# Block-causal attention, MLP and gated convolution on one core: normalization moved behind the value matmul, MLP begun three half pairs earlier

## The chip, the cores and the metric

The kernel runs on one NeuronCore of a Trainium2 chip. The metric is device time in microseconds (us) of one execution. TensorE (PE in the rows; PEld is its weight load) multiplies matrices into PSUM, VectorE is DVE, ScalarE is ACT, GpSimd is POOL, and SP issues most transfers.

## The reference

Three layers follow each other. All outputs of one are inputs of the next.

```python
# attention: B=8, H=8, S=576, D=64, blocks of 64 keys
scores = scale * np.matmul(q, k.transpose(0, 1, 3, 2))
scores = np.where(block_i >= block_j, scores, -1000000000.0)
attn = np.exp(scores - np.max(scores, axis=-1, keepdims=True))
attn = attn / (np.sum(attn, axis=-1, keepdims=True) + 1e-09)
x = np.matmul(attn, v)                    # heads side by side: 8 x 576 x 512
# MLP, with a token mix of rank 32 ahead of it
u = x + (x.transpose(0, 2, 1) @ U @ V).transpose(0, 2, 1)
x = u + np.maximum(u @ w_ch1, 0.0) @ w_ch2          # 512 -> 2048 -> 512
# gate: causal convolution of 5 taps per channel
gate = 1.0 / (1.0 + np.exp(-gate_pre))
out = (gate * (x @ w_val)) @ w_out
```

The weights are float64, q, k and v are float32.

## The kernel before

*Precision.* A product that must be near fp32 is made of three one-pass products of fp32r parts (high x high, high x low, low x high). `hi_act` and `lo` make such parts. Attention matmuls of the first heads are plain fp32.

*Weight conversions.* `split_w1` and `split_w2` fetch a 512 KB piece of a float64 weight (two staging buffers), join its two words by four VectorE operations (lines 122, 124, 125 and 143), and split the result on ScalarE and GpSimd (lines 91 and 97). There are 32. During the first part of the program one is issued every 12 steps; what is left is issued in MLP group 0, four at its first slice and two at each that follows. Pieces of `w_ch2` go back to DRAM and are loaded again per slice.

*The stream of attention.* `attention()` is a generator whose steps the main loop takes one by one. Its first 16 heads (batches 0 and 1) run in 16 half-pair *slots*. A pair is two heads of a batch; `z` holds the pair's queries block-diagonally, so that a 128-column block `i` of it gives, in one matmul against the keys `tk`, the scores of 64 queries of either head. Half 0 of a pair has the query blocks 6 to 8, half 1 the blocks 0 to 5. In `slot(u)`:

- `emit_q_bank(u, b)` for b = 0, 1, 2 makes the scores of a PSUM tile (line 445), their row maxima on VectorE (447), scales these by -1/8 (459), and lets ScalarE take the exponentials with their row sums (463). Block 8 has 576 keys and lies in two tiles, so its first tile waits for the maximum of the second.
- `emit_q_norm(u)` adds 1e-9 (473), takes reciprocals (474), and multiplies the rows of exponentials by them (479): blocks 0 to 5 on VectorE, 6, 7 and 8 on GpSimd.
- `emit_q_turn(u - 1, b)` turns the normalized rows with TensorE (500) and copies them to SBUF on ScalarE (503).
- `emit_q_pv(u - 2, part)` multiplies the values by them (526), part 0 between banks 0 and 1, part 1 between banks 1 and 2; ScalarE copies the result, the pair's transposed output `xt`, from PSUM (534).
- `mix_T`, `mix_G` and `mix_H2` turn `xt` and add the token mix; they make `uh` and `ul`, which the MLP reads.

From head 16 on, `tick(n)` handles one late head: scores with keys on partitions (`emit_s_piece`, 406), maxima over partitions and a subtraction (593 to 631), exponentials (655), and two ticks later the values (`emit_pv`, 719). From `FIRST_SPLIT` on, a head's exponentials are split into high and low parts (`emit_est`); these use pools that open when all conversions are issued (`open_late`).

*The MLP.* 4608 tokens are nine groups of 512, each of 16 slices of the 2048 hidden features. A slice is 12 matmuls of 512 columns for the hidden layer (946), ScalarE's ReLU and VectorE's remainder (974, 975), and 12 matmuls into four accumulators (998). Group g needs the outputs of batches 0 to g. After every six MLP matmuls `gap()` may take steps from the attention stream; `aim(g)` sets how many, by a count of steps over 60 of the group's 64 gaps. Where the stream yields true, a group's share ends; if it has not come by the group's end, the rest is taken at once, without MLP work between (lines 1192 to 1194).

*Where the MLP begins.* With `BREAK = 15`, slots 0 to 15 run ahead of it. Group 0 then carries the 12 steps that finish pairs 6 and 7; from group 1 on the late heads run between the MLP's matmuls.

*What sets the order.* TensorE's order is that of the program. The other engines' order is chosen by the scheduler, in which parts marked `high_priority` go first. Score tiles and half of the transposed tiles share a ring of four PSUM buffers, tag `a`, before the MLP; inside the MLP a single ring of four holds these, the value tiles, the mix and the hidden layer.

Of the kernel before, what the change touches and what calls it, by code (L numbers as in the profile page):

```python
# [17 lines left out]
P = 128  # L18
# [4 lines left out]
def attn_moe_gate_kernel(ctx: ExitStack, tc: tile.TileContext, q, k, v, U, V, w1, w2, wval, convw, wout, out):  # L23
# [21 lines left out]
    FIRST_SPLIT = 2 * H  # L45
# [31 lines left out]
    BREAK = 2 * H - 1  # L77
    ONVEC = (0, 1, 2, 3, 4, 5)
# [142 lines left out]
    make_identity(nc, ident)  # L221
    unit = const.tile([KC, KC], F32, name="unit")
# [171 lines left out]
    def emit_s_piece(pn, i):  # L394
# [15 lines left out]
        for n, t in zip(heads, ps):  # L410
# [23 lines left out]
    def emit_q_bank(u, b):  # L434

        pn, g = divmod(u, 2)
        z, tk = qkt[pn]
        if b == 0:
            t = tiny_p.tile([P, 24], F32, tag="rq", name="rq")
            halves[u] = [t[:, 6 * c:6 * c + 6] for c in range(4)] + [None]  # L440
        r, nm, l, _, wait = halves[u]
        ps = psum["a"].tile([P, 512], F32, tag="a", name="pS")
        todo = qbanks[g][b]
        for i, k0, k1, o, c in todo:
            pe.matmul(ps[:, o:o + k1 - k0], z[:, i * P:(i + 1) * P], tk[:, k0:k1], start=True, stop=True)
        for i, k0, k1, o, c in todo:
            vec.reduce_max(r[:, c:c + 1], ps[:, o:o + k1 - k0], axis=AX.X)
        if g == 0 and b == 0:
            halves[u][4] = ps
            return  # L450
        c0, c1 = todo[0][4], todo[-1][4] + 1
        todo = [(ps, x) for x in todo]
        if wait is not None:
            vec.tensor_tensor(r[:, 0:1], r[:, 0:1], r[:, 1:2], op=ALU.max)
            vec.tensor_copy(r[:, 1:2], r[:, 0:1])
            c0 = 0
            todo = [(wait, qbanks[0][0][0])] + todo
# [35 lines left out]
    def emit_q_turn(u, b):  # L493
# [9 lines left out]
        act.copy(e, ps[:, 0:c])  # L503
        turned[u, b] = e

    def emit_q_pv(u, part):

        pn, g = divmod(u, 2)
        if part == 0 and g == 0:
            xts[pn] = x_p.tile([P, S], F32, tag="xt", name="xt")  # L510
        xt = xts[pn]
        i0, i1 = half_i[g]
        if part == 0:
            turned[u] = ps_p.tile([P, 512], F32, tag="a", name="pPV")
# [18 lines left out]
        if part == 1:  # L533
            act.copy(xt[:, i0 * D:i1 * D], turned.pop(u)[:, 0:(i1 - i0) * D])
            last[0] = (own[0], xt[own[0]][0:1, i0 * D:i0 * D + 1])

    def slot(u):
# [32 lines left out]
        for step, delay in ((mix_H2, 6), (mix_G, 5), (mix_T, 4)):  # L570
            pn, off = divmod(u - delay, 2)
            if off == 0 and 0 <= pn < 2 * NP:
# [3 lines left out]
                yield u >= NQ and step is mix_H2 and pn == 2 * NP - 1  # L576
# [308 lines left out]
    def attention():  # L885
# [10 lines left out]
        for n in range(NQ, NH + DEPTH + HPOS // 2):  # L896
            yield from tick(n, 2 * NP)
# [375 lines left out]
```

## Time and profile before

| | us |
|---|---|
| median of 3 runs (1484.11 to 1488.53) | 1486.95 |
| the profiled execution | 1485.87 |
| its span, first to last instruction | 1484.0 |
| TensorE busy | 1405.5 (95%) |
| VectorE busy | 1054.6 (71%) |
| ScalarE busy | 702.2 (47%) |
| GpSimd busy | 329.3 (22%) |

A busy share is a mean over stages with different limits. Matmuls overlap, so their durations add up to more than the busy time. In the program the first hidden-layer matmul starts at 162.2 us, group 1 begins at about 280 us and group 2 at about 441 us.

### The profile page before, as it was taken

The page shows a single profiled execution, that of the slowest core. Times are in us where ns is not written, and L with a number is a line of the kernel's source. Part 1 is how long each engine was busy: PE and PEld are TensorE (multiplying, and loading weights), DVE is VectorE, ACT ScalarE, POOL GpSimd, SP SyncE. Part 2 cuts the span into 40 slices and gives each one's busy share as a digit, 9 for nine tenths or more (in the row PEclk, how much of TensorE's full clock was granted, in tenths as well). Part 3 has the DMA queues.
Part 4 walks back from the last instruction along what each step waited for, and adds up shares of the span by engine and source line. Part 5 has one row for each costly group of instructions (what it writes and reads, how often), then busy time and mean ns, then how long its engine had stood idle before and what let it go on. Part 6 is the DMA issues. An engine that isn't in the chain of part 4 may idle for free.

```text
span 1484.0 us, 20191 instructions
## 1 busy us (share of the span) xinstructions
PE 1405.5 (95%) x6736; PEld 1087.3 (73%) x6736; DVE 1054.6 (71%) x2215; ACT 702.2 (47%) x1545; POOL 329.3 (22%) x442
## 2 busy tenths in 40 slices
PE   4787898999979999999999999999999999999999
PEld 3454676767757777777777777777888888878887
DVE  5888777598887888787677868886323326399991
ACT  2566543365566555556555555555322222344342
POOL 2444333211121112111221211121112100343310
PEclk8999999999999999999999999999999999999999
DMA  4444577434323344333333434332245533223311
GB/s 87 118 120 98 168 249 248 147 81 112 85 57 95 87 109 124 81 96 85 109 96 87 102 110 90 94 99 75 78 155 166 160 117 125 100 72 100 103 60 66
DMA packets 246290, 163.58 MB, mean 110 GB/s; under 512 B 197669, under 2 KB 212261, under 8 KB 246186
## 3 DMA queue, kind: packets, MB, share of 16 engines
q1 hardware_dynamic: 246186, 162.29, 39.0%
q8 instruction: 54, 0.88, 0.3%
q14 instruction: 50, 0.41, 0.1%
HBM read 134.98 MB, written 27.26 MB: 109 GB/s over the span
## 4 chain that ended last, share of the span: by engine, by line
PE 77%; DVE 8%; DMA 4%; ACT 2%; issue 1%; POOL 1%; SPq 0%; ACTq 0%; DVEq 0%; POOLq 0%
PE acc L998 24%; PE h L946 23%; PE pPV L719 7%; PE o L1112 7%; PE val L1088 6%; PE pS L406 5%; DMA raw<-in_moe_w_ch_dram 3%; DVE wa L125 1%; PE pG L795 1%; DMA y_s<-y 1%; PE acc L991 1%; DVE wa L143 1%; ACT wa L120 1%; PE pT L779 1%; DVE m L595 1%
## 5 line engine op out<-in xcount | busy, mean ns | idle before, releaser
L998 PE MATMUL acc<-hh,w 128*128 128x512 f32 x1152 | 400.2, 402 | 2.9 <-ACT hh L974 2.1
L998 PEld LDWEIGHTS acc<-hh,w 128*128 128x128 f32 x1152 | 218.5, 190 | 69.6 <-issue 21.1
L998 PE MATMUL acc<-hl,w 128*128 128x512 f32 x576 | 227.8, 396 | 8.2 <-DVE hl L975 8.1
L946 PE MATMUL h<-uh,w1hi 128*128 128x512 f32 x576 | 234.2, 407 | 0.0
L946 PE MATMUL h<-uh,w1lo 128*128 128x512 f32 x576 | 225.6, 392 | 0.0
L946 PE MATMUL h<-ul,w1hi 128*128 128x512 f32 x576 | 225.2, 391 | 0.0
L975 DVE SCALAR_TENSOR_TENSOR hl<-h,hh 128x512 fp32r<-128x512 f32 x144 | 98.5, 684 | 130.2 <-ACT hh L974 129.0
L974 ACT ACTIVATE hh<-h 128x512 fp32r<-128x512 f32 x144 | 85.8, 596 | 186.1 <-PE h L946 178.2
L97 POOL TENSOR_TENSOR vlo<-vstk,vhi 128x320 fp32r<-128x320 f32 x48 | 44.7, 932 | 443.6 <-ACT vhi L91 398.2
L946 PEld LDWEIGHTS h<-uh,w1hi 128*128 128x128 f32 x576 | 108.3, 188 | 41.0 <-issue 18.0
L998 PEld LDWEIGHTS acc<-hl,w 128*128 128x128 f32 x576 | 109.5, 190 | 30.6 <-DVE hl L975 11.5
L946 PEld LDWEIGHTS h<-uh,w1lo 128*128 128x128 f32 x576 | 108.1, 188 | 23.8
L946 PEld LDWEIGHTS h<-ul,w1hi 128*128 128x128 f32 x576 | 108.4, 188 | 18.8
L1070 DVE SCALAR_TENSOR_TENSOR gt<-yb,cw,gt 128x516 f32<-128x516 f32 (+1 forms) x144 | 115.2, 831 | 1.4
L406 PE MATMUL pS<-tq,tk 64*128 64x320 f32 (+4 forms) x576 | 100.2, 432 | 5.7 <-ACT za L411 4.0
L97 POOL TENSOR_TENSOR yl<-yb,yh 128x512 fp32r<-128x512 f32 (+7 forms) x64 | 66.8, 1078 | 107.4 <-ACT yh L91 107.3
L411 ACT COPY s<-pS 128x320 f32<-128x320 f32 (+2 forms) x128 | 59.9, 497 | 45.8 <-PE pS L406 42.6
L97 POOL TENSOR_TENSOR ul<-xt,uh 128x512 fp32r<-128x512 f32 (+7 forms) x64 | 55.9, 879 | 103.3 <-ACT uh L91 103.2
L406 PEld LDWEIGHTS pS<-tq,tk 64*128 64x128 f32 x576 | 46.3, 187 | 42.9 <-issue 21.3
L655 ACT ACTIVATE s<-s 128x448 f32<-128x448 f32 x64 | 45.2, 711 | 53.5 <-DVE s L631 53.3
L631 DVE TENSOR_TENSOR s<-s,mb 128x64 f32<-128x64 f32 (+4 forms) x160 | 68.1, 489 | 0.4
L500 PE MATMUL pE<-ident,s 128*128 128x128 f32 x200 | 32.3, 307 | 31.6 <-POOL s L479 22.0
(177 smaller groups left out, 2738.4 us busy)
## 6 DMA issues: line engine op xcount, KB each, us to landing
w<-w_s SPq DMA_DIRECT2D x144, 512.0 KB, 3.3
rawq<-in_q_dram SPq DMA_DIRECT2D x128, 72.0 KB, 2.6
rawk<-in_k_dram SPq DMA_DIRECT2D x128, 72.0 KB, 2.8
out_dram<-ot SPq DMA_DIRECT2D x35, 256.0 KB, 2.0
vstk<-in_v_dram SPq DMA_DIRECT2D x64, 128.0 KB, 2.5
raw<-in_moe_w_ch_dram SPq DMA_DIRECT2D x64, 128.0 KB, 2.3
raw<-in_moe_w_ch_dram SPq DMA_DIRECT2D x16, 512.0 KB, 3.8
w_s<-wo SPq DMA_DIRECT2D x16, 512.0 KB, 3.5
```

The lines of the kernel that those rows point to most:

```text
L97: eng.tensor_tensor(o, i, f32(h), op=ALU.subtract)
L406: pe.matmul(t[:, o:o + w], tk[me, kslice(j)], tq[me, a0:a1], start=True, stop=True)
L411: act.copy(stt[n][half_of[j]][:, d:d + o], t[:, 0:o])
L631: noted(3, vec.tensor_tensor(sv(n, j), sv(n, j), mb[:, q0[j]:], op=ALU.subtract))
L719: pe.matmul(o_, l_, r_, start=(i == 0), stop=(i == len(todo) - 1))
L946: pe.matmul(ps[:, 0:n], w[:, d, fs], x[:, d, 0:n], start=(d == 0 and i == 0), stop=(d == ND - 1 and i == 2))
L974: act.activation(hh[:, 0:n], ps[:, 0:n], AF.Relu)
L975: latest[0] = vec.scalar_tensor_tensor(hl[:, 0:n], ps[:, 0:n], 0.0, f32(hh[:, 0:n]), op0=ALU.max, op1=ALU.subtract)
L998: pe.matmul(acc[d][:, 0:n], w[:, wi, ds], x[:, 0:n], start=False, stop=(f == NF - 1 and i == 2))
L1070: vec.scalar_tensor_tensor(gt[d][:, 0:gw], y[:, d, j:j + gw], cw[:, d, j:j + 1], gt[d][:, 0:gw], op0=ALU.mult, op1=ALU.add)
L1088: pe.matmul(ps[:, 0:n], w[:, d, es], x[:, d, 0:n], start=(i == 0), stop=(i == 3 * ND - 1))
L1112: pe.matmul(ps[:m, cs], x[:, e, a:a + m], w[:, e, cs], start=(i == 0), stop=(i == 3 * ND - 1))
```

## The change

1. Keys of the first 16 heads are multiplied by 1/8 on GpSimd once they are transposed, so that scores come scaled. The maxima are reduced with their sign turned, and the operations that scaled and copied them go.
2. The exponentials stay unnormalized. GpSimd sums up, adds 1e-9 and, after the reciprocals, writes a matrix `fold x reciprocal` into `xt`: row (head, q) has its reciprocal in column q of each block. A matmul with `both`, ones within each head's 64 x 64 corner, spreads the reciprocals over the head's 64 output rows (`emit_q_spread`). ScalarE copies that to `xt`; the values then go into the same PSUM tile, and VectorE multiplies the two into `xt`.
3. All value matmuls of a slot stand between banks 1 and 2. One of seven copies of turned tiles per pair moves from ScalarE to VectorE.
4. `BREAK = 12`: 13 half pairs go ahead of the MLP. Group 0 carries the steps of slots 13 to 20 and four late heads (16 to 19); the stream yields true there. `aim(0)` counts 58 steps.
5. Heads 16 and 17 keep whole fp32 exponentials (`FIRST_SPLIT = 18`).

```diff
-    FIRST_SPLIT = 2 * H
+    FIRST_SPLIT = 2 * H + 2
-    BREAK = 2 * H - 1
+    BREAK = H + 4
+    EARLY = 4
...
+    pool.tensor_tensor(fold, ident[:, 0:P // 2], ident[:, P // 2:], op=ALU.add)
...
+        pool.memset(both[64 * a:64 * a + 64, 64 * a:64 * a + 64], 1.0)
...
+            pool.tensor_scalar(tk, tk, scale, None, op0=ALU.mult)
             qkt[pn] = (z, tk)
...
-            vec.reduce_max(r[:, c:c + 1], ps[:, o:o + k1 - k0], axis=AX.X)
+            x = vec.tensor_reduce(nm[:, c:c + 1], ps[:, o:o + k1 - k0], axis=AX.X, op=ALU.max, negate=True)
...
-        x = vec.tensor_scalar(nm[:, c0:c1], r[:, c0:c1], -scale, None, op0=ALU.mult)
...
     def emit_q_norm(u):
...
-        for bank in qbanks[g]:
-            for i, k0, k1, o, c in bank:
-                if k0 == 0:
-                    w = D * (i + 1)
-                    (vec if i in ONVEC else pool).tensor_scalar(eblk[i][:, 0:w], eblk[i][:, 0:w], rec[:, c:c + 1], None, op0=ALU.mult)
+        pool.tensor_tensor(
+            xts[pn][:, i0 * D:i1 * D].rearrange("p (i q) -> p i q", q=D),
+            fold.rearrange("p (o q) -> p o q", o=1).to_broadcast([P, n, D]),
+            rec[:, 0:n].rearrange("p (i o) -> p i o", o=1).to_broadcast([P, n, D]),
+            op=ALU.mult,
+        )
+
+    def emit_q_spread(u):
...
+        ps = turned[u] = ps_p.tile([P, 512], F32, tag="a", name="pPV")
+        pe.matmul(ps[:, 0:n], both, xs, start=True, stop=True)
+        act.copy(xs, ps[:, 0:n])
...
-            act.copy(xt[:, i0 * D:i1 * D], turned.pop(u)[:, 0:(i1 - i0) * D])
+        vec.tensor_tensor(xt[:, i0 * D:i1 * D], ps[:, 0:(i1 - i0) * D], xt[:, i0 * D:i1 * D], op=ALU.mult)
...
-                emit_q_pv(u - 2, 0)
+                emit_q_spread(u - 2)
...
-                emit_q_pv(u - 2, 1)
+                emit_q_pv(u - 2)
...
-                yield u >= NQ and step is mix_H2 and pn == 2 * NP - 1
+                yield False
...
+            if n == NQ + EARLY:
+                yield True
...
-            count = 12
+            count = 34 + 6 * EARLY
```

The order on TensorE, slot 3, ahead of the MLP. Before (`mb`, `lt` and `t` hold the turned exponentials of blocks 0 to 5, `vstk` the values of the two heads):

```order
L445 MATMUL pS<-tk,zb 128x384
L445 MATMUL pS<-tk,zb 128x128
L526 MATMUL pPV<-mb,vstk_152 64x256
L526 MATMUL pPV<-mb,vstk_153 64x256
L526 MATMUL pPV<-lt,vstk_152 64x128
L526 MATMUL pPV<-lt,vstk_153 64x128
L526 MATMUL pPV<-lt,vstk_152 64x128
L526 MATMUL pPV<-lt,vstk_153 64x128
L445 MATMUL pS<-tk,zb 128x320
L445 MATMUL pS<-tk,zb 128x192
L526 MATMUL pPV<-t,vstk_152 64x256
L526 MATMUL pPV<-t,vstk_153 64x256
```

And now, in the same slot:

```order
L452 MATMUL pS<-tk,zb 128x384
L452 MATMUL pS<-tk,zb 128x128
L496 MATMUL pPV<-xt,both 128x384
L452 MATMUL pS<-tk,zb 128x320
L452 MATMUL pS<-tk,zb 128x192
L543 MATMUL pPV<-mb,vstk_158 64x256
L543 MATMUL pPV<-mb,vstk_159 64x256
L543 MATMUL pPV<-lt,vstk_158 64x128
L543 MATMUL pPV<-lt,vstk_159 64x128
L543 MATMUL pPV<-lt,vstk_158 64x128
L543 MATMUL pPV<-lt,vstk_159 64x128
L543 MATMUL pPV<-t,vstk_158 64x256
```

A spreading matmul stands where the first six value matmuls stood; these have moved behind the next score bank.

The order on GpSimd, about one pair in the middle of the slots. Before (`s` are rows of exponentials, `ul`, `wo` and `w1lo` low parts of the mix and the weights):

```order
L479 TENSOR_SCALAR s_156<-s_156,rq 128x576
L479 TENSOR_SCALAR s_158<-s_158,rq 128x448
L479 TENSOR_SCALAR s_157<-s_157,rq 128x512
L97 TENSOR_TENSOR ul<-xt,uh 128x512
L97 TENSOR_TENSOR ul<-xt,uh 128x64
L97 TENSOR_TENSOR wo<-wa,wo 128x512
L479 TENSOR_SCALAR s_156<-s_156,rq 128x576
```

And now:

```order
L475 TENSOR_TENSOR rq<-rq 128x1
L476 TENSOR_SCALAR rq<-rq 128x3
L482 TENSOR_TENSOR xt<-fold,rq 128x192
L97 TENSOR_TENSOR ul<-xt,uh 128x512
L97 TENSOR_TENSOR ul<-xt,uh 128x64
L97 TENSOR_TENSOR wo<-wa,wo 128x512
L97 TENSOR_TENSOR w1lo<-wa,w1hi 128x4x128
L476 TENSOR_SCALAR rq<-rq 128x6
L387 TENSOR_SCALAR tk<-tk 128x576
L482 TENSOR_TENSOR xt<-fold,rq 128x384
```

The three multiplications of 448 to 576 columns are gone; in their place stand operations on 1, 3 or 6 columns, two products of 192 and 384 columns, and one scaling of 576 columns of keys.

The order on TensorE where the MLP begins (`h` is the hidden layer). Before, after the transposes of slot 15:

```order
L500 MATMUL pE<-ident,s_156 128x128
L500 MATMUL pE<-ident,s_158 128x128
L500 MATMUL pE<-ident,s_157 128x128
L500 MATMUL pE<-ident,s_156 128x128
L795 MATMUL pG<-x,ust_150 128x256 x5
L946 MATMUL h_1725<-uh,w1hi 128x512
L946 MATMUL h_1725<-ul,w1hi 128x512
L946 MATMUL h_1725<-uh,w1lo 128x512
L946 MATMUL h_1725<-uh,w1hi 128x512
L946 MATMUL h_1725<-ul,w1hi 128x512
L946 MATMUL h_1725<-uh,w1lo 128x512
L526 MATMUL pPV<-m,vstk_152 64x192
```

And now, after the mix of slot 12:

```order
L834 MATMUL pH<-vst,g 128x512
L834 MATMUL pH<-vst,g 128x64
L795 MATMUL pT<-ident,xt 128x128 x4
L803 MATMUL pT<-ident,xt 64x128
L964 MATMUL h_1385<-uh,w1hi 128x512
L964 MATMUL h_1385<-ul,w1hi 128x512
L964 MATMUL h_1385<-uh,w1lo 128x512
L964 MATMUL h_1385<-uh,w1hi 128x512
L964 MATMUL h_1385<-ul,w1hi 128x512
L964 MATMUL h_1385<-uh,w1lo 128x512
L452 MATMUL pS<-tq,za 128x384
L452 MATMUL pS<-tq,za 128x128
```

The first hidden-layer matmuls now follow the last mix of batch 0, and the scores of slot 13 stand behind six of them.

## Rows read from the trace of the kernel before

**Rows 1.** Busy time by stage: stretch, us, then each engine's (count), clock granted, DMA.
```profile
0.00:29.00 29.00, 10.49 (x34) 7.10 (x35) 15.78 (x38) 8.00 (x25) 9.34 (x23) 0.88 0.59 102
29.00:131.00 102.00, 78.81 (x490) 50.09 (x490) 82.00 (x238) 60.99 (x190) 38.94 (x30) 0.95 0.45 109
131.00:162.00 31.00, 23.53 (x148) 16.39 (x147) 24.58 (x70) 20.43 (x63) 15.49 (x11) 0.95 0.44 105
162.00:280.00 118.00, 105.58 (x471) 81.36 (x471) 86.03 (x128) 47.85 (x92) 38.90 (x33) 0.97 0.68 223
280.00:441.00 161.00, 150.57 (x738) 112.90 (x737) 132.17 (x306) 90.98 (x193) 28.99 (x58) 0.99 0.37 91
441.00:1080.00 639.00, 636.38 (x3104) 491.80 (x3105) 480.80 (x1076) 346.06 (x732) 112.82 (x202) 0.99 0.36 95
1080.00:1484.00 404.00, 400.17 (x1761) 327.70 (x1760) 233.24 (x360) 127.90 (x253) 84.82 (x86) 1.00 0.34 111
```

**Rows 2.** Groups of TensorE, 29 to 131 us: count | busy, mean ns | idle before, releasers.
```profile
L500 PE MATMUL pE<-ident,s 128*128 128x128 f32 x136 | 20.9, 294 | 16.3 <-POOL s L479 11.0 <-ACT s L463 4.5 <-ACT mb L503 0.7
...
L445 PE MATMUL pS<-tq,za 128*128 128x512 f32 (+7 forms) x48 | 16.3, 452 | 1.5 <-ACT s L463 1.3
...
L526 PE MATMUL pPV<-e,vstk 128*64 128x192 f32 x72 | 8.6, 346 | 1.3 <-ACT e L503 1.3
...
L526 PE MATMUL pPV<-m,vstk 128*64 128x192 f32 (+1 forms) x48 | 4.4, 311 | 3.2 <-ACT m L503 3.2
```

**Rows 3.** TensorE in order of time, one pair: start, us, work [idle before].
```profile
94.31 0.66 PE L500 MATMUL pE<-ident,s 128*128 128x128 f32 x4 [1.35 <-ACT s L463]
...
102.29 1.53 PE L500 MATMUL pE<-ident,s 128*128 128x128 f32 x12 [1.38 <-POOL s L479]
...
104.25 1.02 PE L445 MATMUL pS<-tk,zb 128*128 128x512 f32 x2
```

**Rows 4.** All engines in order of time, the start.
```profile
21.57 4.75 POOL L479 TENSOR_SCALAR s<-s,rq 128x576 f32<-128x576 f32 x3 [16.39 <-DVE rq L474]
...
24.84 0.47 PE L500 MATMUL pE<-ident,s 128*128 128x128 f32 x1 [6.00 <-POOL s L479]
...
26.38 2.82 PE L500 MATMUL pE<-ident,s 128*128 128x128 f32 x12 [1.07 <-POOL s L479]
```

**Rows 5.** TensorE in order of time, end of group 1.
```profile
431.73 1.22 PE L795 MATMUL pG<-x,ust 128*128 128x256 f32 x4 [5.18 <-DVE x L97]
```

**Rows 6.** Groups of GpSimd by shape, 29 to 162 us.
```profile
L479 POOL TENSOR_SCALAR s<-s,rq 128x576 f32<-128x576 f32 x7 | 12.4, 1776 | 44.9 <-ACT t L503 24.7 <-DVE rq L474 15.3 <-ACT x L91 4.9
...
L97 POOL TENSOR_TENSOR w1lo<-wa,w1hi 128x512 fp32r<-128x512 f32 x4 | 5.2, 1290 | 10.8 <-ACT w1hi L91 10.8
```

**Rows 7.** Busy time of line 406 (scores of late heads), group 1.
```profile
280.00:441.00 161.00, 28.46 (x161) 14.28 (x161) 0.99 0.37 91
```

**Rows 8.** Busy time of line 719 (values of late heads), group 1.
```profile
280.00:441.00 161.00, 28.23 (x150) 24.79 (x150) 0.99 0.37 91
```

**Rows 9.** Groups of VectorE, 162 to 280 us: the weight conversions.
```profile
L125 DVE SCALAR_TENSOR_TENSOR wa<-raw,wa 128x512 uint32<-128x512 uint32 x24 | 26.6, 1107 | 0.7
...
L143 DVE SCALAR_TENSOR_TENSOR wa<-raw,wa 128x512 uint32<-128x512 uint32 x24 | 18.8, 783 | 0.4
...
L122 DVE TENSOR_SCALAR wa<-wa 128x512 f32<-128x512 f32 x24 | 14.5, 604 | 20.9 <-ACT wa L120 20.9
...
L124 DVE TENSOR_SCALAR wa<-wa 128x512 uint32<-128x512 uint32 x24 | 10.2, 424 | 0.5
```

**Rows 10.** Groups of VectorE by shape, 70 to 141 us.
```profile
L125 DVE SCALAR_TENSOR_TENSOR wa<-raw,wa 128x512 uint32<-128x512 uint32 x5 | 3.6, 729 | 0.1
```

**Rows 11.** Chain of work, 160 to 290 us: start, us, what.
```profile
168.59 2.36 DMA raw<-in_moe_w_ch_dram
...
254.43 3.12 DMA raw<-in_moe_w_ch_dram
...
265.71 2.73 PE h L946 x12
```

More of the change, by code (lines that the diff above doesn't have):

```diff
@@ L221, in attn_moe_gate_kernel @@
     make_identity(nc, ident)
+    fold = ac_p.tile([P, P // 2], F32, name="fold")
+    pool.tensor_tensor(fold, ident[:, 0:P // 2], ident[:, P // 2:], op=ALU.add)
+    both = ac_p.tile([P, P], F32, name="both")
+    pool.memset(both, 0.0)
+    for a in range(2):
+        pool.memset(both[64 * a:64 * a + 64, 64 * a:64 * a + 64], 1.0)
     unit = const.tile([KC, KC], F32, name="unit")
@@ L438, in emit_q_bank @@
         if b == 0:
-            t = tiny_p.tile([P, 24], F32, tag="rq", name="rq")
-            halves[u] = [t[:, 6 * c:6 * c + 6] for c in range(4)] + [None]
-        r, nm, l, _, wait = halves[u]
+            t = tiny_p.tile([P, 18], F32, tag="rq", bufs=3, name="rq")
+            halves[u] = [t[:, 6 * c:6 * c + 6] for c in range(3)] + [None]
+        nm, l, _, wait = halves[u]
         ps = psum["a"].tile([P, 512], F32, tag="a", name="pS")
@@ L462, in emit_q_bank @@
         for src, (i, k0, k1, o, c) in todo:
-            act.activation(eblk[i][:, k0:k1], src[:, o:o + k1 - k0], AF.Exp, bias=nm[:, c:c + 1], scale=scale, accum_out=l[:, c:c + 1])
+            m = 2 if i == NI - 1 else c
+            act.activation(eblk[i][:, k0:k1], src[:, o:o + k1 - k0], AF.Exp, bias=nm[:, m:m + 1], scale=1.0, accum_out=l[:, c:c + 1])
     def emit_q_norm(u):
         g = u % 2
-        r, nm, l, rec, _ = halves.pop(u)
-        n = 6
+        nm, l, rec, _ = halves.pop(u)
+        n = 6 if g else 3
         if g == 0:
-            vec.tensor_tensor(l[:, 0:1], l[:, 0:1], l[:, 1:2], op=ALU.add)
-            n = 4
-        vec.tensor_scalar(l[:, 0:n], l[:, 0:n], 1e-9, None, op0=ALU.add)
+            pool.tensor_tensor(l[:, 2:3], l[:, 3:4], l[:, 2:3], op=ALU.add)
+        pool.tensor_scalar(l[:, 0:n], l[:, 0:n], 1e-9, None, op0=ALU.add)
         vec.reciprocal(rec[:, 0:n], l[:, 0:n])
-        for bank in qbanks[g]:
-            for i, k0, k1, o, c in bank:
-                if k0 == 0:
-                    w = D * (i + 1)
-                    (vec if i in ONVEC else pool).tensor_scalar(eblk[i][:, 0:w], eblk[i][:, 0:w], rec[:, c:c + 1], None, op0=ALU.mult)
+        pn = u // 2
+        if g == 0:
+            xts[pn] = x_p.tile([P, S], F32, tag="xt", name="xt")
+        i0, i1 = half_i[g]
+        pool.tensor_tensor(
[5 more added lines that the diff above has]
+    def emit_q_spread(u):
+        pn, g = divmod(u, 2)
+        i0, i1 = half_i[g]
+        n = (i1 - i0) * D
+        xs = xts[pn][:, i0 * D:i1 * D]
+        ps = turned[u] = ps_p.tile([P, 512], F32, tag="a", name="pPV")
+        pe.matmul(ps[:, 0:n], both, xs, start=True, stop=True)
+        act.copy(xs, ps[:, 0:n])
     def turn_space(g, b):
@@ L502, in emit_q_turn, with emit_q_pv @@
         e = turn_space(g, b)[:, 0:c]
-        act.copy(e, ps[:, 0:c])
+        if g and b == 2:
+            vec.tensor_copy(e, ps[:, 0:c])
+        else:
+            act.copy(e, ps[:, 0:c])
         turned[u, b] = e
-    def emit_q_pv(u, part):
+    def emit_q_pv(u):
         pn, g = divmod(u, 2)
-        if part == 0 and g == 0:
-            xts[pn] = x_p.tile([P, S], F32, tag="xt", name="xt")
         xt = xts[pn]
         i0, i1 = half_i[g]
-        if part == 0:
-            turned[u] = ps_p.tile([P, 512], F32, tag="a", name="pPV")
-        ps = turned[u]
+        ps = turned.pop(u)
         n = len(tbanks[g])
-        for b in range(n)[(0, 2)[part]:(2, n)[part]]:
+        for b in range(n):
             c = 0
@@ L532, in emit_q_pv @@
                     )
-        if part == 1:
-            act.copy(xt[:, i0 * D:i1 * D], turned.pop(u)[:, 0:(i1 - i0) * D])
-            last[0] = (own[0], xt[own[0]][0:1, i0 * D:i0 * D + 1])
+        vec.tensor_tensor(xt[:, i0 * D:i1 * D], ps[:, 0:(i1 - i0) * D], xt[:, i0 * D:i1 * D], op=ALU.mult)
+        last[0] = (own[0], xt[own[0]][0:1, i0 * D:i0 * D + 1])
     def slot(u):
```

22 lines of the change are left out of this document (9 added, 13 removed).

## The prediction

> **What bounds the kernel now.** I read the busy time of each stage first, because the 95% of TensorE over the whole span says nothing about one stage. The table of stages [rows 1] shows three regimes. From 441 us on TensorE is busy 636.4 of 639 us and then 400.2 of 404 us: nothing the change touches can gain there, and it edits no work there. The idle time sits ahead of that: 18.5 us before 29 us (29.0 - 10.5), 23.2 us in 29 to 131 us (half-pair slots 2 to 12), 7.5 us in 131 to 162 us (slots 13 to 15), 12.4 us in 162 to 280 us (MLP group 0) and 10.4 us in 280 to 441 us (group 1). That is 72.0 of the 78.5 us in which TensorE does nothing. The kernel is TensorE-bound with a badly filled front, so a gain means: less idle time before 441 us, against whatever TensorE work is added.
>
> Then I asked what ended those idle times. In the slots [rows 2] the transposes wait 11.0 us for GpSimd's multiplications of the exponentials, 4.5 us for exponentials and 0.7 us for a copy on ScalarE; the value matmuls wait 1.3 + 3.2 us for the copies of transposed weights; scores wait 1.3 us. With 0.9 us not shown here these are the 23 us. In the timeline of one pair [rows 3] the two kinds repeat: 1.35 us for an exponential (a PSUM buffer not yet read) and 1.38 us for GpSimd. At the start [rows 4] GpSimd's three multiplications take 4.75 us and hold TensorE for 6.00 + 1.07 us. At the end of group 1 the stream of attention steps is not finished and is drained with no MLP work between: one wait alone is 5.18 us [rows 5].
>
> **The change part by part.**
>
> *Start, slot 0 and 1.* The waits of 6.00 + 1.07 us go [rows 4], since the transposes read the exponentials as ScalarE leaves them. New on the path: the first keys are scaled by GpSimd before the first score. A 576-wide multiplication took GpSimd 1.78 us [rows 6]; ends 0 (were it hidden) and 1.78. I take 1.8, as nothing stands between transpose and score: -7.1 + 1.8 = -5.3 us. Later keys are scaled a pair ahead and cost nothing; without that cover, 1.8 us a pair.
> The Trainium skill, GPSIMD Engine Reference, section Engine selection, says one-input operations run roughly at line rate there and two-input ones about twice as slow. The rows say otherwise: one input, 576 wide, 1776 ns; two inputs, 512 wide, 1290 ns [rows 6], so the measured row decides. By the page, half of 1290 x 576/512, some 0.7 us (an estimate), the start would gain 1.1 us more.
>
> *Slots 2 to 12.* Gone: GpSimd's 11.0 us, outright. The 4.5 us of value matmuls (1.3 + 3.2) go too, because these matmuls now all stand behind the second score bank of 512 columns, 1.0 us later. The 4.5 + 1.3 + 0.7 us on ScalarE I also count as gone: VectorE loses its six multiplications and four or five scaling operations per pair, so the maxima on which the exponentials wait come sooner. Added: a spreading matmul of 192 or 384 columns in each slot; 512 columns of fp32 took 1.02 us [rows 3], so a pair's 576 cost 1.15 us, 0.57 us a slot, 6.3 us for 11 slots. Also new is a wait: the value matmuls write the PSUM tile that ScalarE must have copied out, and behind them in TensorE's queue stand the third bank and the transposes. No row shows it. Below nothing is excluded, it removes no work; the lower end is 0, the upper the dearest similar wait per slot, 1.35 us [rows 3]. I take 0.5, since that score bank stands between. So 102 us becomes 78.8 busy + 6.3 + 5.5 = 90.6: -11.4 us. The MLP would begin near 29.0 - 5.3 + 90.6 = 114 us.
>
> *Slots 13 to 15 and group 0.* Together they took 31 + 118 = 149 us. TensorE's work in the new group 0: 105.6 [rows 1], 23.5 of the three slots, five spreadings at 0.57 = 2.9, the scores of four heads and the values of two. Group 1 held 161 score matmuls in 28.46 us [rows 7], 12 a head, so 13.4 heads at 2.12 us; 150 value matmuls in 28.23 us [rows 8], 15 a head, 10 heads at 2.82 us. Heads 16 and 17 take their exponentials whole in fp32: 1600 columns at 1.02 us per 512 is 3.2, so 2.8 to 3.2, and I take 3.0. Together 4 x 2.12 + 2 x 3.0 = 14.5. Sum 146.5 us. Idle time: at least 12.4 as now, and more, because VectorE's load climbs. It was 86.0; add two weight conversions that the shorter front leaves over (their four operations: 70.1 us for 24 [rows 9], 2.9 each), at most 24.6 of the slots, and at most 9.9 a head (132.2 over 13.4 heads, everything in that stage included): 156 us at most. Its share goes from 73% to about 92%, so I double the idle time and round: 23.5, group 0 = 170 us. Ends 10 and 45. Moved: +21 us for the two stages.
>
> *Group 1.* Leaves: four heads' scores 8.5 and two heads' values 5.6 us. The drain also shrinks: by the code some 92 stream steps were to fit 72 (64 gaps at 68/60); now 72 remain. Of 10.4 us idle I leave 4: 161 - 14.1 - 6.4 = 140.5, -20.5 us. What is late next is the last mix of a batch, now in the last gap with nothing spare; hence the 4.
>
> *Free edits.* The extra GpSimd setup lies in the wait for the first queries. The small additions and the 16 products on GpSimd stand in a queue that was busy 38.9 of 102 us [rows 1]; the matrix they make is wanted a slot later. Without this cover a slot would wait for one product, up to 1290 x 384/512 = 970 ns [rows 6]. After 441 us: 0.
>
> *Sum.* -5.3 - 11.4 + 21.0 - 20.5 = -16.2 us on the profiled execution's 1485.87 us: 1469.7. The median shown is 1.1 us above that execution, so **1471 us**.
>
> **The rivals.**
>
> *Front keeps its rhythm.* If only GpSimd's waits go and every ScalarE wait is kept (6.5 + 4.5 us instead of the 5.5 allowed), slots 2 to 12 take 96.1 us, and the time is 1476. For: exponentials, not GpSimd, end half the waits [rows 3]. Against: VectorE, their releaser, is relieved.
>
> *VectorE and GpSimd slow each other in group 0.* The conversion's two-input operation takes 729 ns among the slots [rows 10] and 1107 ns in group 0 [rows 9], where GpSimd subtracts two inputs at once. If the heads' operations stretch as much, up to 4 x 9.9 x 0.52 = 20 us of VectorE time come in; half of it reaching TensorE gives 1481.
> The Trainium skill, GPSIMD Engine Reference, section Key points, states this contention for VectorE instructions with two SBUF inputs; the 729 against 1107 ns agrees, and it speaks against moving more of both engines' work into one stage.
>
> *VectorE's queue sets group 0: slower than before.* The conversions wait on loads: VectorE idled 20.9 us for them in group 0 [rows 9], which hurt little, as only the hidden layer's remainders stood behind. Rounds of two conversions ran 8.6 us apart (ten from 168.6 to 254.4 us [rows 11]). Now the reductions of three slots and the chains of four heads stand behind those waits in program order, and behind them TensorE, whose score and transposed tiles share four PSUM buffers with the hidden layer. If VectorE's 156 us are all needed and its idle time grows with the conversions from 32.0 (118 - 86.0) to 34.7, plus some 10 us in the last two slices that hold no attention (5.5 us each: twelve matmuls of the hidden layer took 2.73 us [rows 11], the twelve of the accumulators are counted alike), group 0 takes 201 us: 1502. It decides for slower from 186 us on, that is 30 us of VectorE idle time. Against: at most 156 us are counted, and work of the last heads may run over into group 1.
>
> *The change only moves idle time.* Group 0 idles about 38 us and the rest happens as forecast: 1486, no change.
>
> **How the numbers follow.** A measurement of this kernel can tell about 0.3%, 4.5 us, from no change. Chances: forecast 0.55 (its own range 1455 to 1480), front keeps its rhythm 0.14, contention 0.10, better than the forecast (no new wait, group 0 idling 10 us: 1452) 0.05, idle time only moved 0.07, VectorE's queue 0.09. The first four give faster, less 0.04 for two of them coming together: 0.80. Of that 0.03 falls to same, 0.10, and 0.01 to slower, 0.10. The range 1450 to 1488 leaves out the slow rival and a tail at either end.
>
> **What would show it.** The first hidden-layer matmul near 114 us (not 162); no wait for GpSimd ahead of the transposes; slots of about 8.2 us; the first accumulator copies near 284 us, after a group 0 of 165 to 175 us; group 1's idle time under 5 us. Wrong: a begin after 121 us refutes the front's term, a group 0 above 180 us that of its idle time, and then VectorE and the hidden remainders must show as releasers; a wait above 1 us a slot of value matmuls for the spread copy refutes the cover.

## The result, and the profile after

The changed kernel takes 1445.69 us (median of 4 runs, 1443.84 to 1447.4) where the kernel before, run beside it, took 1487.53: a ratio of 0.9722, 95% interval 0.9702 to 0.9743, or 42 us less. The prediction was 1471, in a range of 1450 to 1488. The way it moved was right, the gain was 2.6 times as large as forecast, and the time lies 4 us below the range.

The stages of the changed kernel (one profiled execution, 1447.4 us, span 1445.6) are cut where slot 2 begins, at the first hidden-layer matmul, at the first accumulator copy of group 0, at that of group 1, and at 1042 us. The columns are those of [rows 1]: the stretch, its length, busy time (count) of PE, PEld, DVE, ACT and POOL, TensorE's granted clock, DMA.

```profile
0.00:20.10 20.10, 9.45 (x33) 5.73 (x34) 10.06 (x20) 5.91 (x19) 9.24 (x28) 1.00 0.67 117
20.10:109.50 89.40, 76.79 (x520) 53.84 (x521) 75.70 (x184) 61.97 (x197) 38.03 (x51) 0.98 0.59 132
109.50:273.20 163.70, 143.80 (x679) 105.91 (x680) 135.03 (x259) 81.00 (x180) 53.64 (x59) 0.95 0.64 186
273.20:412.70 139.50, 138.39 (x682) 106.05 (x681) 105.42 (x238) 77.49 (x164) 24.04 (x49) 1.00 0.36 95
412.70:1042.00 629.30, 628.65 (x3093) 487.56 (x3092) 472.50 (x1055) 339.81 (x720) 110.91 (x196) 1.00 0.37 97
1042.00:1445.60 403.60, 399.81 (x1760) 327.41 (x1758) 233.19 (x360) 127.84 (x253) 84.85 (x86) 1.00 0.33 111
```

Group 1 of the kernel before was cut in [rows 1] at 280 and 441 us. By its accumulator copies it runs from 277.9 to 449.8 us. The same view of the kernel before, re-cut, with its last 29.8 us alone:

```profile
277.90:449.80 171.90, 159.74 (x761) 118.21 (x760) 140.82 (x325) 98.21 (x206) 31.89 (x65) 0.97 0.36 88
...
420.00:449.80 29.80, 20.63 (x86) 13.75 (x85) 27.77 (x62) 18.71 (x42) 10.40 (x19) 0.81 0.22 48
```

Where the time went, stage by stage:

| stage | before | after | moved | forecast |
|---|---|---|---|---|
| start | 29.0 | 20.1 | -8.9 | -5.3 |
| slots 2 to 12 | 102.0 | 89.4 | -12.6 | -11.4 |
| slots 13 to 15 and group 0 (131 to 277.9) | 146.9 | 163.7 | +16.8 | +21.0 |
| group 1 | 171.9 | 139.5 | -32.4 | -20.5 |
| rest | 1034.2 | 1032.9 | -1.3 | 0 |

The stages add up to 38.4 us, the difference of the two profiled spans (1484.0 and 1445.6); that of the medians is 42. Against the forecast of 16.2 us the stages gained 22.2 us more, and 11.9 of these are group 1's, the large miss. Over the whole span TensorE's busy time fell from 1405.5 to 1396.9 us, though the change gives it work to do. So busy time is not work here: the granted clock rose from 0.986 to 0.993 in the mean, and a matmul takes longer at the lower level. That turns out to be part of the miss.

In the slots of the changed kernel no transpose waits for GpSimd's multiplication any more. All that TensorE waited for between 20.1 and 109.6 us (the view of waits: engine, tile, line, releaser: us in total, times, longest) is:

```profile
PE pPV L543 <- ACT xt L497: 5.4, 4, 2.0
PE pE L518 <- ACT s L467: 3.4, 2, 1.9
PE pT L803 <- ACT lt L524: 2.9, 4, 1.1
PE pS L452 <- ACT s L467: 0.6, 1, 0.6
PE pPV L496 <- DVE xt L836: 0.6, 1, 0.6
PE pH L834 <- DVE vst L97: 0.3, 1, 0.3
```

The first row is the wait that the prediction had to bound without a row: the value matmuls behind ScalarE's copy of the spread reciprocals. It is 5.4 us, where 5.5 were allowed; that is 0.5 us a slot over 11 slots, though it came in four waits of up to 2.0 us.

### The profile page after: what moved, and what is told of

It reads as the page before. It is cut to its first block, busy times and chain, and to the rows that moved or that the text cites. A ratio compares the mean times of both kernels' runs of the same rounds, so it can differ in the third digit from the quotient of the medians.

```text
span 1445.6 us, 20118 instructions
## 1 busy us (share of the span) xinstructions
PE 1396.9 (97%) x6762; PEld 1086.5 (75%) x6762; DVE 1031.9 (71%) x2113; ACT 694.0 (48%) x1529; POOL 320.7 (22%) x468
## 4 chain that ended last, share of the span: by engine, by line
PE 83%; DVE 6%; DMA 5%; ACT 3%; SPq 1%; issue 1%; POOL 0%; ACTq 0%; DVEq 0%; POOLq 0%
PE h L964 26%; PE acc L1016 25%; PE pPV L735 8%; PE o L1130 7%; PE val L1106 7%; PE pS L413 6%; DMA raw<-in_moe_w_ch_dram 4%; PE pG L811 1%; DVE wa L125 1%; PE acc L1009 1%; PE pS L452 1%; ACT s L467 1%; DVE wa L143 1%; PE pT L795 1%; ACT wa L120 1%
## 5 line engine op out<-in xcount | busy, mean ns | idle before, releaser
L964 PE MATMUL h<-uh,w1hi 128*128 128x512 f32 x576 | 238.3, 414 | 4.9 <-ACT s L418 3.5
L993 DVE SCALAR_TENSOR_TENSOR hl<-h,hh 128x512 fp32r<-128x512 f32 x144 | 98.5, 684 | 132.7 <-ACT hh L992 131.5
L964 PEld LDWEIGHTS h<-uh,w1hi 128*128 128x128 f32 x576 | 109.5, 190 | 48.3 <-issue 20.2
L97 POOL TENSOR_TENSOR vlo<-vstk,vhi 128x320 fp32r<-128x320 f32 x46 | 41.8, 908 | 458.3 <-ACT vhi L91 432.0
L671 ACT ACTIVATE s<-s 128x448 f32<-128x448 f32 (+1 forms) x62 | 43.8, 711 | 61.5 <-DVE s L647 61.3
L97 DVE TENSOR_TENSOR el<-s,eh 128x448 fp32r<-128x448 f32 (+1 forms) x62 | 47.4, 798 | 18.2 <-PE pPV L735 10.6
```

The source lines that it names most:

```text
L97: eng.tensor_tensor(o, i, f32(h), op=ALU.subtract)
L964: pe.matmul(ps[:, 0:n], w[:, d, fs], x[:, d, 0:n], start=(d == 0 and i == 0), stop=(d == ND - 1 and i == 2))
L993: latest[0] = vec.scalar_tensor_tensor(hl[:, 0:n], ps[:, 0:n], 0.0, f32(hh[:, 0:n]), op0=ALU.max, op1=ALU.subtract)
```

## The experiments

### The change in its two halves

**norm_only**: normalization alone; the MLP begins after slot 15 and no late head is in group 0.

```diff
-    FIRST_SPLIT = 2 * H + 2
+    FIRST_SPLIT = 2 * H
...
-    BREAK = H + 4
-    EARLY = 4
+    BREAK = 2 * H - 1
...
-            if n == NQ + EARLY:
-                yield True
...
-            count = 34 + 6 * EARLY
+            count = 12
```

> The new normalization alone: 16 slots ahead of the MLP, 12 steps in group 0, no late head there. Theory A (two parts that add up: the normalization shortens the front, the late heads in group 0 end the bare drain behind group 1): the MLP begins near 137 us (162.2 less 8.9 at the start and 1.15 us a slot over 14 slots), group 1 still ends in a drain, and the time is about 1462 us. Theory B (nearly all of the gain is the earlier begin of the MLP; normalization and late heads only move work): the MLP begins after 150 us and the time is above 1475 us.

Measured: 1460.28 us, ratio 0.9817 (0.9801 to 0.9833). The MLP begins at 132.7 us, group 0 takes 120.4 and group 1 171.8 us.

**order_only**: the kernel before with the new order alone.

```diff
-    FIRST_SPLIT = 2 * H
+    FIRST_SPLIT = 2 * H + 2
...
-    BREAK = 2 * H - 1
+    BREAK = H + 4
+    EARLY = 4
...
+            if n == NQ + EARLY:
+                yield True
...
-            count = 12
+            count = 34 + 6 * EARLY
```

> The old normalization with the new order: 13 half pairs ahead of the MLP, four late heads in group 0, heads 16 and 17 whole. Theory A: the MLP begins near 131 us as slot 12 ended before, group 0 takes 164 to 170 us, group 1 about 140 us without a drain, time about 1472 us. Theory B: 1455 us or less, as the begin of the MLP is three half pairs earlier.

Measured: 1469.78 us, 0.9882 (0.9866 to 0.9897). The MLP begins at 132.9 us, group 0 takes 161.8 and group 1 139.6 us. In time both runs lie within 3 us of what theory A gave (1462 and 1472); theory B, which wanted 1455 or less from the order alone, falls. The two halves add up: -26.7 and -17.2 us (0.0183 and 0.0118 of the time before) make -43.9, and both together measured -42. So the normalization is the larger half. Group 1 has its new length with the order alone and its old one with the normalization alone.

**no_late**: the change without the four late heads in group 0, and with heads 16 and 17 in two parts again. **late_only**: the kernel before with only these two points of the change (BREAK stays 15).

```diff
# no_late, against the change
-    FIRST_SPLIT = 2 * H + 2
+    FIRST_SPLIT = 2 * H
...
-    EARLY = 4
+    EARLY = 0
# late_only, against the kernel before
-    FIRST_SPLIT = 2 * H
+    FIRST_SPLIT = 2 * H + 2
...
+    EARLY = 4
...
+            if n == NQ + EARLY:
+                yield True
...
-            count = 12
+            count = 12 + 6 * EARLY
```

> The changed kernel with no late head in group 0 (its share there 34 steps; all late heads' exponentials in two parts as before). Theory A: begin at 109.5 us as in the changed kernel, group 0 about 149 us, group 1 again about 172 us with a drain of some 28 us in which no MLP matmul stands; time about 1463 us, 17 us over the changed kernel. Theory B: within 4 us of the changed kernel's 1446 us.

> The kernel before with only the four late heads moved into group 0 (16 slots ahead of the MLP, old normalization, heads 16 and 17 whole). If the stages' lengths add, group 0 grows by 25 us (no_late against the changed kernel: 138.4 to 163.7) and group 1 falls by 32 us to 139.5: time about 1480 us. If late heads fit into group 0 only because slots 13 to 15 leave VectorE idle between their waits, group 0 grows by over 32 us and the time is 1487 us or more.

Measured: no_late 1455.83 us, 0.9786 (0.9769 to 0.9803), so the four heads are worth some 10 us in the change, between the texts' two numbers; late_only 1474.36 us, 0.9932 (0.9909 to 0.9955), so they are worth as much (0.0068) in the kernel before, where adding up the stages had given 7 us. In no_late group 0 takes 138.4 us (the text had about 149) and group 1 171.6 us; with the heads moved they take 163.7 and 139.5. Moving four heads costs group 0 25.3 us and gives group 1 32.1. By the prediction their TensorE work is 14.1 us. What else in group 1 is worth 18?

### What holds group 1

**paced**: the kernel before, with group 1 taking its stream's steps faster, so that nothing is left to drain at its end. If the drain is the loss, it goes.

```diff
-            pace[:] = [0.0, (count if g == 0 else 8 * H + NP) / (4.0 * NF - SPARE), 0]
+            pace[:] = [0.0, (count if g == 0 else 96 if g == 1 else 8 * H + NP) / (4.0 * NF - SPARE), 0]
```

> The kernel before, with one number changed: group 1 takes steps at 96 to 60 gaps instead of 68, so that its 92 steps end inside the group and none is left for the drain. The work is the same. Theory A (a drain without MLP work costs, by waits, by the halved clock and by matmuls that stand alone): group 1 shortens from 172 to about 160 us, time about 1475 us. Theory B, and a third, C (VectorE, 88% busy in 160 us, bounds group 1 however the steps lie): within 4 us of 1487 us.

Measured: 1486.41 us, 0.9994 (0.9981 to 1.0006): no change, so theory A, the drain, falls. The drain is gone, group 1 is 173.5 us long, and TensorE idles in the middle instead. All engines in order of time there, six rows (start, us, what, [idle before <- releaser]):

```profile
301.14 1.16 DVE L631 TENSOR_TENSOR za<-za,mb 128x64 f32<-128x64 f32 x3
302.22 1.02 DVE L631 TENSOR_TENSOR zb<-zb,mb 128x448 f32<-128x448 f32 x2
302.40 0.58 ACT L655 ACTIVATE za<-za 128x448 f32<-128x448 f32 x1 [2.16 <-DVE za L631]
...
303.75 0.84 ACT L655 ACTIVATE zb<-zb 128x768 f32<-128x768 f32 x1
...
304.50 0.51 ACT L411 COPY s<-pS 128x448 f32<-128x448 f32 x1
...
305.06 1.29 PE L406 MATMUL pS<-tq,tk 64*128 64x448 f32 x4 [2.74 <-ACT s L411]
```

TensorE's wait names ScalarE's score copy, but that copy stands in ScalarE's queue behind exponentials, and the first of these had waited 2.16 us for VectorE's subtraction. Around this wait, from 300 to 310 us, VectorE is busy 9.70 of 10 us, and from 320 to 400 us 74.2 of 80 (the third busy time of each row):

```profile
320.00:360.00 40.00, 36.90 (x177) 26.21 (x176) 36.68 (x85) 26.46 (x56) 8.10 (x16) 0.96 0.26 67
360.00:400.00 40.00, 39.70 (x197) 30.65 (x196) 37.51 (x82) 22.48 (x49) 8.06 (x14) 1.00 0.43 94
```

In the kernel before it is as full where the drain stands: 27.77 of the last 29.8 us, in the row shown further up. The releaser of TensorE's wait is ScalarE; the engine that is late is VectorE. What of its work matters was tried next. No pace between 68 and 96 was run.

**sub_pool**: half of the late heads' subtractions on GpSimd, in the kernel before.

```diff
-            noted(3, vec.tensor_tensor(sv(n, j), sv(n, j), mb[:, q0[j]:], op=ALU.subtract))
+            if half == 0:
+                noted(3, vec.tensor_tensor(sv(n, j), sv(n, j), mb[:, q0[j]:], op=ALU.subtract))
+            else:
+                pool.tensor_tensor(sv(n, j), sv(n, j), mb[:, q0[j]:], op=ALU.subtract)
```

> The kernel before, with the subtraction of the second half of each late head's scores (448 and 320 columns, together about 1.0 us on VectorE) given to GpSimd, where two inputs cost some 2.5 ns a column, 1.9 us a head. Theory C (VectorE's work bounds group 1, 140.8 us of 171.9): 13 heads take 13 us off it, group 1 shortens to about 158 us and the time to about 1474 us. Theory A (the drain's bare waits are what is lost): group 1 stays at 172 us or grows by GpSimd's longer latency, time 1485 to 1492 us.

Measured: 1557.83 us, 1.0483 (1.0441 to 1.0525). As a test of VectorE's part it fails, because VectorE was not relieved. Its remaining subtractions, by shape, 460 to 1000 us; first sub_pool, then the kernel before (count | busy us, mean ns):

```profile
L632 DVE TENSOR_TENSOR s<-s,mb 128x576 f32<-128x576 f32 x21 | 27.2, 1293 | 0.0
```

```profile
L631 DVE TENSOR_TENSOR s<-s,mb 128x576 f32<-128x576 f32 x22 | 16.5, 750 | 0.0
```

The same subtraction takes 1293 ns instead of 750 when GpSimd subtracts too, and the one of 192 columns 1244 instead of 351. The three that VectorE keeps of such a head take 2896 ns; all five took 2423. GpSimd needs 1179 ns for its 448 columns and 958 for its 320.

**no_sub**: those subtractions left out for heads 16 to 28, and given to nobody. **paced_no_sub**: the same with group 1 paced as in paced. **paced_aside**: paced, with all subtractions executed, but into a scratch tile, so that no exponential reads their results. **paced_no_subs**: paced, with both halves left out.

```diff
# no_sub, paced_no_sub
-            emit_sub(n, 1)
+            if not 2 * H <= n < 29:
+                emit_sub(n, 1)
# paced_aside
-            noted(3, vec.tensor_tensor(sv(n, j), sv(n, j), mb[:, q0[j]:], op=ALU.subtract))
+            o = sv(n, j)
+            if 2 * H <= n < 29:
+                o = rot("t")[:, q0[j]:]
+            noted(3, vec.tensor_tensor(o, sv(n, j), mb[:, q0[j]:], op=ALU.subtract))
# paced_no_subs
-            emit_sub(n, 0)
-            emit_sub(n, 1)
+            if not 2 * H <= n < 29:
+                emit_sub(n, 0)
+                emit_sub(n, 1)
```

> The kernel before, with the second half's subtraction of the column maxima left out for the late heads 16 to 28 (so this part of the softmax is missing from their result; nothing else is changed, and TensorE's work is the same). That takes about half of the 52 subtractions, 22.1 us, off VectorE's 140.8 us in the 171.9 us of group 1. Theory C (VectorE's chains of 13 heads bound group 1): the group becomes shorter by what VectorE loses, 9 to 14 us, so 158 to 163 us, and the time 1473 to 1478. Theory A (TensorE's own work and waits that have nothing to do with VectorE's load bound it): the group stays within 3 us of 172 and the time within 4 of 1487, since no matmul is taken away. A result between 1478 and 1483 would leave it open.

> The kernel before with group 1's attention steps paced at 96 in place of 68 (alone: 1486.4 us, no drain, group 1 173.5 us long, VectorE 150.0 us busy in it), and the second half's subtraction left out for the late heads 16 to 28 as in no_sub (that part of their softmax is missing). no_sub, with the drain still there, saved 3.2 us of the 9 us that VectorE lost. If VectorE's throughput is what holds the paced group, nearly all of those 9 us come back: group 1 near 164 us, time near 1477, 4 below no_sub. If the loss in group 1 comes from something else, the time stays where no_sub was, 1480 to 1484.

> The kernel before with group 1 paced at 96, and the subtractions of heads 16 to 28 all executed but written to a scratch tile, so that the exponentials read unshifted scores (the shift by the column maxima is missing from their result). VectorE has the same work; what is gone is the exponential's wait for the chain of maxima, transposes and subtractions behind it. If VectorE's throughput holds the group: no change against paced, group 1 170 to 175 us, time 1484 to 1488. If the length of each head's chain holds it, from scores to exponential: the waits for the score buffers' readers on ScalarE and most of the 10.8 us of idle time go, group 1 160 to 165 us, time 1474 to 1479.

> The kernel before with group 1 paced at 96 and both halves' subtractions left out for heads 16 to 28 (the shift by the column maxima is missing from their softmax; the maxima are still worked out). Group 1 took 173.5 us with VectorE 150.0 us busy (paced), 174.3 with 147.9 (paced_aside, the wait gone but the work kept) and 167.0 with 135.7 (paced_no_sub). VectorE should now be busy some 122 to 126 us. If its load goes on setting the length, by about 0.45 us for each of its microseconds as in the last step, the group takes 160 to 163 us and the time is 1473 to 1477. If the 6.5 us were all that VectorE held, the group stays at 165 to 168 us and the time at 1479 to 1482, and the rest of its idle time has another cause. TensorE's own work, at full clock and without a pause, would take at most 152.5 us (138.4 + 14.1).

Measured: no_sub 1480.97 us, 0.9978 (0.9966 to 0.9990); paced_no_sub 1480.43, 0.9963 (0.9949 to 0.9976); paced_aside 1486.9, 0.9999 (0.9988 to 1.0011); paced_no_subs 1465.27, 0.9885 (0.9854 to 0.9917). Group 1 in the view of stages, for paced, paced_aside, paced_no_sub and paced_no_subs in turn:

```profile
279.20:452.70 173.50, 162.75 (x759) 119.39 (x759) 150.04 (x340) 97.42 (x206) 31.61 (x65) 0.96 0.37 88
```

```profile
278.40:452.70 174.30, 161.48 (x760) 119.06 (x759) 147.87 (x341) 98.69 (x208) 31.93 (x65) 0.96 0.36 87
```

```profile
280.10:447.10 167.00, 160.07 (x759) 117.97 (x758) 135.65 (x316) 98.50 (x207) 30.73 (x65) 0.97 0.38 91
```

```profile
274.70:430.10 155.40, 153.13 (x759) 114.80 (x758) 124.69 (x280) 99.02 (x208) 30.11 (x65) 1.00 0.40 98
```

The same 759 matmuls of TensorE stand in 173.5, 167.0 and 155.4 us (paced, paced_no_sub, paced_no_subs), as VectorE's busy time goes from 150.0 to 135.7 to 124.7. ScalarE's stays at 97 to 99. In the last run only 2.3 us of idle time are left, at a granted clock of 1.00. So nearly all of what the group has beyond TensorE's work hangs on VectorE's part of the late heads: it goes when the subtractions go. The first step gave 6.5 us of group 1, the second 11.6 more: the slope rises, which the text on record for the last run had not expected (it said 160 to 163 us; 155.4 came). In time the ratios put paced_no_subs 0.0109 below paced, 16 us, beside the 18.1 us of group 1 in the profiled executions. The results of no_sub (3 us) and paced_no_sub (5.5 us) lay between the theories or at the edge of what the texts had set; the second step decided.

paced_aside was to tell VectorE's load from the exponentials' wait for it. It does not, though its time is what the load theory forecast. The exponential overwrites the scores in place, and the subtraction put aside still reads them, so the exponential waits as before. ScalarE's largest such waits, first in paced, then in paced_aside (engine, tile, line, releaser: us in total, times, longest):

```profile
ACT s L655 <- DVE s L631: 6.8, 5, 2.4
```

```profile
ACT s L658 <- DVE t L634: 15.4, 11, 4.6
```

With those of the tiles `za` and `zb` they are 11.2 us in paced and 20.2 in paced_aside. Leaving a subtraction out shortens VectorE's load and a head's chain of operations alike. That it is the load is therefore argued and not shown. For it speak that VectorE has hardly a pause where TensorE waits (9.70 of 10 us, 74.2 of 80, 27.77 of 29.8), and that the exponentials' waits for VectorE do not follow the group's length: 11.2 us in paced, 15.5 in paced_no_sub, 10.9 in paced_no_subs.

### Smaller terms, and a better version

**spread_first**: the change, with the spreading matmul issued ahead of a slot's first score bank instead of behind it, so that ScalarE's copy has a bank more of time.

```diff
-        if u < NQ:
-            with tc.high_priority():
-                emit_q_bank(u, 0)
-            yield False
         if 0 <= u - 2 < NQ:
             with tc.high_priority():
                 emit_q_spread(u - 2)
             yield False
+        if u < NQ:
+            with tc.high_priority():
+                emit_q_bank(u, 0)
+            yield False
```

> The changed kernel with the spreading matmul ahead of a slot's first score bank instead of behind it. Its copy out of PSUM then has two banks of cover. If the copy is late because it starts late, the value matmuls' 6.4 us of waits for it (five waits of 0.65 to 1.99 us) go and the time falls by 4 to 6 us to about 1441 us. If it is late because ScalarE's queue holds exponentials that wait for maxima, it stays within 2 us of 1446 us.

Measured: 1443.46 us, 0.9721 (0.9704 to 0.9738), no different from the change. The waits for the spread copy in the slots fall from 5.4 to 2.9 us (the text's 6.4 has one of 1.0 us in group 0 besides), and others take their place (a remainder for the mix 2.6 us, where it was 0.3). The copy was not what held the slots.

**scale_vec**: the change, with the first pair's keys scaled on VectorE. **early3** and **early5**: scale_vec with three or five late heads in group 0.

```diff
-            pool.tensor_scalar(tk, tk, scale, None, op0=ALU.mult)
+            (pool if pn else vec).tensor_scalar(tk, tk, scale, None, op0=ALU.mult)
# early3 (early5: 5)
-    EARLY = 4
+    EARLY = 3
```

> The changed kernel with the first pair's keys scaled by VectorE instead of GpSimd. If the first scaling lies on the path, as the first score's wait for GpSimd until 9.96 us says, the MLP and the end come 1.2 to 1.5 us earlier, 1444.5 us. If the start is absorbed by a later wait, no difference.

> The change with the first pair's keys scaled on VectorE (1441.8 us in its own run), and three late heads begun before the accumulation in place of four. A head costs group 0 about 6.3 us (25.3 us for four between the runs with none and with four). If group 1 gains or loses 8 us for each head all the way (171.6 us with none moved, 139.5 with four), it grows to 147.5 and the time is about 1443.5, +1.8. If group 1 with nine heads has slack on VectorE already (TensorE is busy 138.4 of 139.5 us there), the bend lies above four heads moved's load: it grows only by the head's TensorE work, 3.5 us, and the time is about 1439, -2.8.

> The same with five late heads begun early. Group 0 grows by about 6.3 us. TensorE is busy 138.4 of 139.5 us in group 1 with four moved, so only the head's own TensorE work, about 3.5 us, can leave it if TensorE bounds it now: 1444.6, +2.8. If VectorE still bounded it, 8 us would leave it: 1440, -1.8.

Measured: scale_vec 1441.8 us, 0.9707 (0.9690 to 0.9724); early3 1447.1, 0.9747 (0.9726 to 0.9768); early5 1444.91, 0.9739 (0.9722 to 0.9755). In scale_vec the first pair's scaling takes VectorE 0.46 us instead of GpSimd's 1.66, and scores begin at 8.93 us instead of 9.96. First the change, then scale_vec (start, us, what):

```profile
8.24 1.66 POOL L387 TENSOR_SCALAR tq<-tq 128x576 f32<-128x576 f32 x1 [2.36 <-DVE tq L384]
```

```profile
8.32 0.46 DVE L387 TENSOR_SCALAR tq<-tq 128x576 f32<-128x576 f32 x1
```

It has the lowest median here, some 2 us below the change, but the two intervals overlap, so that a gain in time is not shown. early3 and early5 bring nothing. With three heads moved group 0 is 158.9 and group 1 146.7 us long; with four (scale_vec) 159.7 and 139.4; with five 174.8 and 129.0, and TensorE is busy through all of group 1. Four has the lowest time of the three, though the intervals of four and five touch, and neither text got the sizes right for both groups: steps come in pairs of heads (early5's group 1 has 24 score matmuls fewer than the change's, two heads' worth, and early3's has as many as the change's).

## Why the prediction was right in sign and wrong in size

**The step that failed is group 1's term**: "Of 10.4 us idle I leave 4: 161 - 14.1 - 6.4 = 140.5, -20.5 us". The stage fell by 32.4 us. The work that leaves it was sized right: 153.1 us of TensorE with all heads and a full clock (paced_no_subs) against 138.4 after, 14.7 where 14.1 was said. What was mis-sized is the rest of the old group that goes, 6.4 us in the text and 17.7 in the traces:

- Its idle time fell from 12.2 us to 1.1, by 11.1 and not by 6.4 (10.4 to 4). The prediction put it down to a drain, that is, to a count of steps that did not fit. paced made them fit and gained nothing. The cause was VectorE's part of the late heads, 140.8 us busy of 171.9, which the prediction weighed in group 0 and not in group 1. With four heads gone VectorE is busy 105.4 of 139.5 us, and hardly a wait is left.
- Its busy time was taken for work. 159.7 - 153.1 = 6.6 us of it went though no work did, a term that the sum put at nothing. Matmuls were longer at the lower clock level: the first accumulating ones took 582 ns in the last 29.8 us (granted clock 0.81) and 406 from 320 to 400 us (1.00). That all of the 6.6 us is the clock's was not separated.

14.7 + 11.1 + 6.6 = 32.4 us. That the new length came out nearly right (139.5 us, 140.5 forecast) is luck: the group was cut at 441 us and ended at 449.8, and those last 8.8 us of drain were counted as "After 441 us: 0". A start 10.9 us too short met a saving 11.9 us too small.

The kernel before showed the room beforehand. From 441 us on, TensorE's weight loads took 491.8 of 639 us, 77% [rows 1], in a stretch that has no idle time to speak of. In group 1 they took 118.2 of 171.9 us, 69%. At 77% the same loads would fit in 153.6 us, an estimate; paced_no_subs measured 155.4. The Trainium skill, Perfetto Trace Analysis, section Identifying the Most-Contended Engine, says that the share of time in matmuls is no good measure of how near TensorE is to its limit, and that the share of weight loads is a better one. The trace agrees: 93% by the one, 69 against 77% by the other.

**Start** (-5.3, was -8.9). The waits of 6.00 + 1.07 us went [rows 4], and the scaling of the first keys took GpSimd 1.66 us. The first score came at 9.96 us instead of 8.09, the +1.8 of the forecast. Not foreseen: the only wait of scores for an exponential, 3.36 us at 17.1 us in the kernel before, is 0.60 us ahead of slot 2 now, and TensorE was busy 1.0 us less, at a granted clock of 1.00 instead of 0.88. -7.07 - 2.76 + 1.87 - 1.04 = -9.0. By the page weighed there (the Trainium skill, GPSIMD Engine Reference, section Engine selection) the scaling should have taken some 0.7 us, an estimate; the 1.66 measured speaks against it and is near the 1776 ns of [rows 6]. scale_vec, which takes it off GpSimd, began the scores 1.0 us sooner and slot 2 0.55 us sooner (19.56 instead of 20.11 us).

**Slots 2 to 12** (-11.4, was -12.6). Right in sum by two errors: busy 76.8 us where 78.8 + 6.3 was said, idle 12.6 where 5.5 was. The spreading itself was sized fairly, 22 matmul records busy 7.5 us for 6.3, but the granted clock was 0.98 instead of 0.95, and 137 transposes took 17.3 us where 136 took 20.9 [rows 2]. Transposes' waits for exponentials stayed (3.4 us of 4.5), as the rival of the kept rhythm said, and 2.9 us came ahead of the mix's transposes, where no term stood. The case "better than the forecast" came nearest in time (1452) with the wrong reason: a new wait did come, and group 0 idled 19.9 us and not 10.

**Slots 13 to 15 and group 0** (+21, was +16.8). TensorE's busy time was 143.8 us (said 146.5), its idle time 19.9 (said 23.5). The slower rival's sign, 30 us of VectorE idle time, was nearly there, 163.7 - 135.0 = 28.7, but of VectorE's 156 us "at most" only 135.0 came, and TensorE's longest wait was 3.5 us. The contention rival did not come either: the conversion's two-input operation took 933 ns in this stage, less than the 1107 of [rows 9], and the late heads' subtractions of 576 columns 752 ns, no more than the 750 of the kernel before. Where GpSimd subtracted all through the groups, in sub_pool, they took 1293. The Trainium skill (GPSIMD Engine Reference, section Key points) names this contention, for VectorE instructions with two SBUF inputs; sub_pool's trace agrees, 1293 against 750 ns.

**After 441 us** (0, was -1.3 from 449.8): right from the group's real end on; the 8.8 us before it stand in group 1's account.

## What to carry to other kernels

Cut a stage at an event of the program, not at a round time, and judge TensorE in it by what its loads take in a stretch known to be full, not by its busy share: 93% busy hid 19 us (171.9 against 153.1). Where a chain of small operations feeds TensorE, follow a wait back through the queue of the engine that is named, until an engine is found that had hardly any idle time before it; the one that released the wait was here only the messenger. Count a moved piece of work by what it frees on that engine: four heads were 15 us of TensorE and 32 us of group 1, of which group 0 took back 25. And when an edit is to take a wait away, look in its trace whether the wait is gone.

## What the runs showed of the hardware that was not expected

- A stage with VectorE busy 150.0 of its 173.5 us, no more than 86% in the mean, lost 20 us against TensorE's 153.1; with 124.7 of 155.4 (80%) it lost 2.3.
- Moving two-input subtractions from VectorE to GpSimd made VectorE's remaining ones of 576 columns 1.7 times as long (750 to 1293 ns), and the kernel took 72 us longer (a ratio of 1.0483).
- The same one-input multiplication, 128 x 576 in fp32, took 0.46 us on VectorE and 1.66 us on GpSimd.
